# A sigmoid attention with a gated feed-forward: post-sums of the first layers kept in the PSUM banks of products 0 and 1, and two units of products interleaved

## The chip, the core and the metric

The kernel runs on one core of a Trainium2 chip. The metric is the device time of one execution in microseconds; several runs of a kernel are given by their median. A core has TensorE (PE, matmuls into PSUM; PEld is its weight load), VectorE (DVE), ScalarE (ACT), GpSimd (POOL) and SyncE (SP), which here issues all the DMAs. Each engine works through its own queue in order, and semaphores tie the queues together.

## The reference

```python
scores = scale * np.matmul(q, k.transpose(0, 1, 3, 2)) - np.log(S)   # 8 x 12 heads, S = 448, 64 wide
attn = 1.0 / (1.0 + np.exp(-scores))
x = np.matmul(attn, v)                      # brought to 3584 tokens x 768
gate = 1.0 / (1.0 + np.exp(-(x @ w_gate)))  # w_gate, w_val: 768 x 1536
val = x @ w_val
out = gate * val @ w_out                    # w_out: 1536 x 768
```

The feed-forward weights come as 64-bit words and the results are held to the accuracy of fp32.

## The kernel before, in words

**Stages.** The attention runs first (0 to 268.6 us of the span) and leaves x, transposed, in DRAM. Then the first layers (x times w_gate and w_val, 268.6 to 883.7 us), then the second layer (times w_out). Beside them VectorE, ScalarE and GpSimd convert the weights.

**Products.** Both layers work on 2 x 2 blocks with seven products in place of eight (Winograd's form of Strassen). An operand is a sum of blocks, scaled and split into a high and a low fp16 half (`hl`, `hh`, `b`, `whl`), and a product of the first layers is nine matmuls of 128 x 128 by 448 columns: three tiles of the inner dimension, times low-high, high-high and high-low (`product`, L615; matmuls in L625). It fills one of the eight PSUM banks of the pool `un`.

**Units.** A unit is the seven products of one block of w_gate (t = 0) or w_val (t = 1) with one pair of batches. `unit` (L632) gives each product's result to another engine: products 0 and 1 are copied to SBUF by ScalarE (L638, L640); for products 2 and 3 VectorE adds the running sum in SBUF to the bank (u2, u3; `plus`, L610), and GpSimd adds the copy of product 1 to u2 and u3 (u4, c22); products 4, 5 and 6 get one VectorE sum each (c). The four results c and c22 are the blocks of the layer's output. `done` is then called on each: `gate` (L792: ScalarE's sigmoid L794, for two of four a scaling L356) or `value` (L800: gate times value, two on VectorE in L809, two on GpSimd in L811, then a store to DRAM and, two ticks later, ScalarE's row sums of magnitudes, `sum_abs`, L115).

**Visits.** `visits` is a list of (pair of batches, part): four visits with the first four column pairs of the weights (8 units, 56 products each), four with the other two (4 units, 28 products), then the second layers of the four pairs. 48 units in all, 336 products. `a_visit` (L745) calls `tick` after each product; a tick also moves on the loads of the next pair's x (`load_x`), its operands (`split_x`, GpSimd's differences in L326, splits in L356 and L362), the stores, and `beside` (L942): the steps of the weight conversion that a table made from step counts gives to that tick.

**Conversion.** A group of weights is four tiles of words, two steps each (`first`: L218 ScalarE, L199 GpSimd, L200 VectorE; `second`: L209 to L212 VectorE), then its scale, then seven operands (GpSimd's sums in L260, ScalarE's cast in L356, VectorE's rest in L230, the stores). A scale that must hold for all partitions takes the steps of `Scale.steps` (L165): row maximum (`each`, L127), an idle step, a spread by a small matmul (L595), an idle step, the finish. The maximum of the hidden values of the first pair (`OutScale`) is told in the same way at the start of the second layer, where a product is 18 matmuls (`c_visit`, L842).

**Order.** All of this is written out in program order; nothing is moved afterwards. TensorE waits where a bank isn't free, an operand isn't made or a DMA hasn't landed. The weight operands come through a ring of eight buffers (`load_operands`, L426), some of them stay resident in `v` tiles.

## Time and profile before

| | us |
|---|---|
| median of 3 runs (1182.64 to 1185.46) | 1183.63 |
| the profiled execution | 1182.16 |
| its span, first to last instruction | 1180.4 |
| attention | 268.6 |
| first layers, 336 products | 615.1 |
| second layer | 296.7 |
| PE busy / DVE / ACT / POOL | 1135.0 / 872.0 / 644.6 / 628.2 |

The profile is one execution. In its rows an instruction has its line in the kernel, its engine and its operands as out<-in; "idle before" is the engine's time without work ahead of it, and `<-` names what ended that. Matmuls overlap, so the duration of one (353 ns on average) is longer than the distance from one to the next (0.19 us). Of the stages, 490 to 810 us is the part of the first layers in which conversion runs in nearly all ticks.

### The profile page before, as it was taken

The page shows a single profiled execution, that of the slowest core. Times are in us where ns is not written, and L with a number is a line of the kernel's source. Part 1 is how long each engine was busy: PE and PEld are TensorE (multiplying, and loading weights), DVE is VectorE, ACT ScalarE, POOL GpSimd, SP SyncE. Part 2 cuts the span into 40 slices and gives each one's busy share as a digit, 9 for nine tenths or more (in the row PEclk, how much of TensorE's full clock was granted, in tenths as well). Part 3 has the DMA queues.
Part 4 walks back from the last instruction along what each step waited for, and adds up shares of the span by engine and source line. Part 5 has one row for each costly group of instructions (what it writes and reads, how often), then busy time and mean ns, then how long its engine had stood idle before and what let it go on. Part 6 is the DMA issues. An engine that isn't in the chain of part 4 may idle for free.

```text
span 1180.4 us, 20983 instructions
## 1 busy us (share of the span) xinstructions
PE 1135.0 (96%) x7269; PEld 559.0 (47%) x7269; DVE 872.0 (74%) x1414; ACT 644.6 (55%) x1206; POOL 628.2 (53%) x531
## 2 busy tenths in 40 slices
PE   9999999999799999998999898999998999999998
PEld 3434344445355555444545444444554555555554
DVE  4679999634686878888888888887575787686773
ACT  6777577775456656745664555455454335253340
POOL 0255878941574456456444444445477276392850
PEclk9999999999899999999999999999999999999999
DMA  8699788878578637743554789758854786877744
GB/s 291 212 314 332 246 278 273 258 272 271 180 234 280 225 130 264 267 136 106 169 192 151 195 275 302 254 165 276 259 168 146 216 257 203 259 214 235 215 117 152
DMA packets 174251, 265.32 MB, mean 225 GB/s; under 512 B 49216, under 2 KB 150976, under 8 KB 174144
## 3 DMA queue, kind: packets, MB, share of 16 engines
q1 hardware_dynamic: 174144, 263.98, 69.5%
q8 instruction: 57, 0.93, 0.3%
q14 instruction: 50, 0.41, 0.1%
HBM read 182.48 MB, written 81.43 MB: 224 GB/s over the span
## 4 chain that ended last, share of the span: by engine, by line
PE 60%; DVE 15%; POOL 10%; issue 5%; DMA 5%; ACT 4%; SPq 0%; DVEq 0%; POOLq 0%; ACTq 0%
PE un L625 47%; PE av L497 7%; PE sc L472 6%; DVE whl L230 2%; DVE wf L210 2%; POOL wf L260 2%; POOL whl L359 2%; DVE wf L209 2%; DMA v<-ad 2%; DVE wm L211 2%; DVE c L610 1%; POOL v L326 1%; ACT g L794 1%; ACT junk L115 1%; DVE u L610 1%
## 5 line engine op out<-in xcount | busy, mean ns | idle before, releaser
L625 PEld LDWEIGHTS <-A 128*128 128x128 f16 x3024 | 296.2, 98 | 284.5 <-issue 11.0
L625 PE MATMUL un<-b,v 128*128 128x448 f16 x1512 | 310.8, 357 | 15.5 <-ACT p L638 8.2
L625 PE MATMUL un<-b,A 128*128 128x448 f16 x1512 | 304.5, 353 | 5.8 <-DVE c L610 4.1
L625 PE MATMUL un<-hh,A 128*128 128x448 f16 x1008 | 274.3, 354 | 0.0
L625 PEld LDWEIGHTS <-v 128*128 128x128 f16 x1512 | 149.0, 99 | 159.1 <-issue 23.7
L480 ACT ACTIVATE a<-sc,bias 128x896 f32<-128x896 f32 x168 | 169.2, 1008 | 74.9 <-PE sc L472 60.2
L497 PE MATMUL av<-a,v 64*64 64x448 f32 x1344 | 194.6, 540 | 2.8 <-DVE x L514 2.8
L472 PE MATMUL sc<-qk 64*64 64x448 f32 x1344 | 193.3, 539 | 0.4 <-ACT a L480 0.4
L625 PE MATMUL un<-hl,A 128*128 128x448 f16 x504 | 178.3, 354 | 0.0
L610 POOL TENSOR_TENSOR u<-u,p 128x448 f32<-128x448 f32 x48 | 60.0, 1249 | 167.6 <-DVE u L610 135.3
L199 POOL TENSOR_SCALAR wf<-wf 128x384 f32<-128x384 f32 x72 | 41.2, 573 | 183.1 <-ACT wf L218 116.4
L472 PEld LDWEIGHTS sc<-qk 64*64 64x64 f32 x1344 | 66.4, 134 | 77.6 <-issue 63.5
L497 PEld LDWEIGHTS av<-a,v 64*64 64x64 f32 x1344 | 66.5, 133 | 69.1 <-issue 60.8
L115 ACT ACTIVATE junk<-g 128x448 bf16<-128x448 f32 x88 | 50.6, 575 | 77.9 <-DVE g L809 46.8
L794 ACT ACTIVATE g<-c,back 128x448 f32<-128x448 f32 x96 | 62.4, 657 | 48.3 <-DVE c L610 43.8
L326 POOL TENSOR_TENSOR b<-b 128x448 f32<-128x448 f32 x48 | 67.1, 1434 | 38.5 <-DVE hl L362 38.5
L260 POOL TENSOR_TENSOR wf<-wf 128x384 f32<-128x384 f32 x72 | 80.8, 1126 | 0.0
L326 POOL TENSOR_TENSOR v<-v 128x448 f32<-128x448 f32 x48 | 65.8, 1402 | 27.8 <-DVE hl L362 27.8
L610 POOL TENSOR_TENSOR c<-u,p 128x448 f32<-128x448 f32 x48 | 63.1, 1315 | 17.8 <-DVE u L610 15.3
L514 DVE TENSOR_TENSOR x<-av,x 128x448 f32<-128x448 f32 x48 | 29.7, 618 | 49.0 <-ACT x L507 48.4
L811 POOL TENSOR_TENSOR g<-c,g 128x448 f32<-128x448 f32 x44 | 57.3, 1317 | 13.7 <-DVE c L610 13.2
L610 DVE TENSOR_TENSOR c<-un,u 128x448 f32<-128x448 f32 x96 | 57.5, 614 | 8.6 <-PE un L625 5.3
(343 smaller groups left out, 1476.4 us busy)
## 6 DMA issues: line engine op xcount, KB each, us to landing
A<-ad SPq DMA_DIRECT2D x168, 192.0 KB, 3.6
A<-oo SPq DMA_DIRECT2D x168, 192.0 KB, 2.7
qk<-qk SPq DMA_DIRECT2D x23, 896.0 KB, 5.4
h<-g SPq DMA_DIRECT2D x88, 224.0 KB, 2.3
ad<-whl SPq DMA_DIRECT2D x84, 192.0 KB, 4.1
bd<-b SPq DMA_DIRECT2D x30, 448.0 KB, 3.7
b<-bd SPq DMA_DIRECT2D x30, 448.0 KB, 5.8
v<-vv SPq DMA_DIRECT2D x24, 448.0 KB, 4.5
```

The source lines that it names most:

```text
L115: nc.scalar.activation(junk[:, :x.shape[-1]], x, AF.Abs, accum_out=to)
L199: nc.gpsimd.tensor_scalar(out=f, in0=f, scalar1=F32_MAX, scalar2=F64_ZERO, op0=ALU.min, op1=ALU.max)
L260: nc.gpsimd.tensor_tensor(out=x, in0=y, in1=z, op=op)
L326: engine.tensor_tensor(out=to, in0=x, in1=y, op=ALU.subtract)
L472: nc.tensor.matmul(sc[halves[u], h, :S], lhsT=qkt[halves[h], p, k0:k0 + HP], rhs=qkt[halves[h], p, :S], start=True, stop=True)
L480: nc.scalar.activation(a, sc[:, :, :S], AF.Sigmoid, bias=bias, scale=scale)
L497: nc.tensor.matmul(avs[key][halves[h], :S], lhsT=vt[halves[u], g, h], rhs=a[halves[u], h], start=start, stop=g == last)
L514: nc.vector.tensor_tensor(out=x, in0=other, in1=x, op=ALU.add)
L610: engine.tensor_tensor(out=to, in0=x, in1=y, op=ALU.add)
L625: nc.tensor.matmul(acc, lhsT=w, rhs=m, start=i == 0, stop=i == len(terms) - 1)
L794: nc.scalar.activation(gates[i], acc, AF.Sigmoid, scale=units[0])
L811: nc.gpsimd.tensor_tensor(out=h, in0=acc, in1=gates[i], op=ALU.mult)
```

## The change

`unit` becomes a generator that yields after each product. Product 0 opens a bank, `run`; after ScalarE has copied it (p1), product 2 is added by TensorE to the same bank, and ScalarE copies the sum (u2). Product 3 is added to it in turn, and product 6 at last, so that `run` holds the last result itself, which `done` reads from PSUM. Product 1 opens a bank `side`; product 5 is added to it. Product 4 has a bank of its own. Three results take one VectorE sum each: product 4 with p1, `run` after product 3 with p5, `side` after product 5 with u2. GpSimd makes no post-sums. The products of a unit come in the order 0, 1, 2, 4, 3, 5, 6.

`first_layers` takes the units of all visits as one sequence, in which a unit starts seven places after the one before and takes every second place: two units alternate, over the ends of the visits too. The gating, the row sums and the stores are asked for one product later than they were, the loads of x are spread over more ticks, the splits begin one tick earlier, the maximum's spread has one idle step more, and the second layer's start follows that. `Operands` now makes casts as soon as their scale is there.

```diff
--- before.py
+++ after.py
-TAIL = 12
+TAIL = 13
...
+ORDER = (0, 1, 2, 4, 3, 5, 6)
+APART = 2
...
         def steps(self):
-            return [self.rows, idle, self.spread, idle, self.finish]
+            return [self.rows, idle, idle, self.spread, idle, self.finish]
...
-        return 8 * n_groups + lag + (TAIL + 1 if everywhere else TAIL - 2)
+        return 8 * n_groups + lag + (TAIL + 1 if everywhere else TAIL - 3)
...
+    units = [(v_, jp, t) for v_, (kind, _, part) in enumerate(visits) if kind == "A" for jp in JPS_OF_PARTS[part] for t in range(2)]
+    sequence = [(u, at) for _, u, at in sorted((N_OPS * u + APART * at, u, at) for u in range(len(units)) for at in range(N_OPS))]
+    first_unit = [next(u for u, (w_, *_) in enumerate(units) if w_ == v_) for v_ in range(n_a)]
+    starts = [sequence.index((u, 0)) for u in first_unit] + [len(sequence)]
+    def unit_operand(u, at):
+        v_, jp, t = units[u]
+        n, r, part = ORDER[at], N_OPS * (u - first_unit[v_]) + at, visits[v_][2]
+        return (a_dram[jp][t][n].rearrange("p a f -> p (a f)"), [("a", jp, t, n)],
+                (part, r) if resident(part, r) and v_ < n_a - 1 else None)
...
-    wanted = [x for v_ in range(len(visits)) for x in visit_operands(v_)]
+    wanted = [unit_operand(*x) for x in sequence] + [x for v_ in range(n_a, len(visits)) for x in visit_operands(v_)]
     ring, residents, new_resident = [], {}, [None]
...
-    def product(parts):
-        acc = un.tile([P, 512], F32, tag="un", name="un")[:, :S]
+    def product(parts, acc=None):
+        begin = acc is None
+        if begin:
+            acc = un.tile([P, 512], F32, tag="un", name="un")[:, :S]
...
         for i, (w, m) in enumerate(terms):
-            nc.tensor.matmul(acc, lhsT=w, rhs=m, start=i == 0, stop=i == len(terms) - 1)
+            nc.tensor.matmul(acc, lhsT=w, rhs=m, start=begin and i == 0, stop=i == len(terms) - 1, skip_group_check=not begin)
         load_operands()
         after()
         return acc
...
-    def unit(tick, done):
-        def next_product(n):
-            return product([("p (a k f) -> p a k f", [bs[n, k] for k in range(KC)])])
-        p1, p5, u2, u3, u4, c22 = (sb(n) for n in SUMS[:6])
-        nc.scalar.copy(p1, next_product(0))
-        tick()
-        nc.scalar.copy(p5, next_product(1))
-        tick()
-        plus(u2, next_product(2), p1)
-        plus(u4, u2, p5, nc.gpsimd)
-        tick()
-        plus(u3, next_product(3), u2)
-        plus(c22, u3, p5, nc.gpsimd)
-        tick()
-        c = sb(next(cs))
-        plus(c, next_product(4), p1)
-        done(0, c)
-        later.append(lambda: done(3, c22))
-        tick()
-        c = sb(next(cs))
-        plus(c, next_product(5), u4)
-        done(1, c)
-        tick()
-        c = sb(next(cs))
-        plus(c, next_product(6), u3)
-        done(2, c)
-        tick()
+    copies = {n: itertools.cycle(tags) for n, tags in {0: ("p1", "u3"), 1: ("p5", "u4"), 2: ("u2", "c22")}.items()}
+    def unit(b, done):
+        def next_product(n, acc=None):
+            return product([("p (a k f) -> p a k f", [b[n, k] for k in range(KC)])], acc)
+        def copy(n, acc):
+            c = sb(next(copies[n]))
+            nc.scalar.copy(c, acc)
+            return c
+        def sum_of(acc, x):
+            c = sb(next(cs))
+            plus(c, acc, x)
+            return c
+        run = next_product(0)
+        p1 = copy(0, run)
+        yield
+        side = next_product(1)
+        p5 = copy(1, side)
+        yield
+        next_product(2, run)
+        u2 = copy(2, run)
+        yield
+        done(0, sum_of(next_product(4), p1))
+        yield
+        next_product(3, run)
+        done(3, sum_of(run, p5))
+        yield
+        next_product(5, side)
+        done(1, sum_of(side, u2))
+        yield
+        next_product(6, run)
+        done(2, run)
+        yield
...
+        def casts(self, to):
+            while self.cast < min(to, len(self.items)) and self.items[self.cast][:2] in outs:
...
+        def rests(self, at):
+            self.casts(at + 1)
...
-            if 2 <= p < 14 or p >= 14 and p % 2 == 0:
-                next(x_loads, None)
-            if p >= 31:
-                next(splits, None)
-            next(moves, None)
+            if 2 <= p < 20 and p % 3 != 0 or p >= 20:
+                next(self.x_loads, None)
+            if p >= 30:
+                next(self.splits, None)
+            if p == N_OPS and self.keep:
+                self.moves = hold(self.pr, self.jps)
+            if p >= N_OPS:
+                next(self.moves, None)
...
-                    unsent.append((p + 3, h_dram[(pr,) + at], h))
+                    unsent.append((clock[0] + 4, h_dram[(pr,) + at], h))
...
-                unsummed.append((p + 2, h, 4 * at[1] + at[0]))
+                unsummed.append((clock[0] + 3, h, h_sums[pr][:, c:c + 1]))
...
+    def first_layers():
+        going, visit = {}, None
+        for u, at in sequence:
+            v_, jp, t = units[u]
+            if at == 0:
+                if u in first_unit:
+                    if visit:
+                        visit.end()
+                    visit = Visit(v_)
+                going[u] = visit.begin(jp, t)
+            next(going[u])
+            clock[0] += 1
+            send_and_sum()
+            visit.tick()
+        clock[0] += 4
+        send_and_sum()
+        visit.end()
...
-            own = [[], own[1:3], own[3:]]
+            own = [[], [], own[1:4], own[4:]]
```

In the built program ScalarE has 48 instructions more, VectorE and GpSimd 96 fewer each, TensorE and SyncE as many as before. The spread of the maximum of w31 comes after 18 products, before after 17, and the row maximum stands earlier by one to two products.

VectorE, near the end of the fourth visit, before. `un` is a bank, `u2`, `u3` and `u4` the running sums, `p1` a copy, `c` a result, `g` a gate, `w` and `o1s` belong to the weight conversion:

```order
L610 TENSOR_TENSOR u2_7898<-un_7940,p1_7896 128x448
L230 SCALAR_TENSOR_TENSOR whl_7925<-wf_7730,o1s_208,whl_7925 128x384
L209 TENSOR_SCALAR wf_7914<-wf_7914 128x384
L210 SCALAR_TENSOR_TENSOR wf_7914<-wraw_7827,wf_7914 128x384
L211 SCALAR_TENSOR_TENSOR wm_7919<-wraw_7827,wm_7919 128x384
L212 SCALAR_TENSOR_TENSOR wf_7914<-wm_7919,wf_7914 128x384
L610 TENSOR_TENSOR u3_7899<-un_7960,u2_7898 128x448
L610 TENSOR_TENSOR c1_7974<-un_7975,p1_7896 128x448
L809 SCALAR_TENSOR_TENSOR g0_7846<-c1_7974,back3_3315,g0_7846 128x448
L230 SCALAR_TENSOR_TENSOR whl_7958<-wf_7447,o1s_208,whl_7958 128x384
L200 TENSOR_SCALAR wm_7996<-wraw_7923 128x384
L610 TENSOR_TENSOR c0_8004<-un_8005,u4_7900 128x448
```

Every product from 2 on has a bank of its own and a VectorE row that reads it: u2, u3, c1, c0, with the conversion's rows between.

A few products on, at the start of the fifth visit, after. `un_7541` is the bank `run` of one unit, `un_7584` its bank `side`, `un_7791` the bank of product 4 of the unit interleaved with it:

```order
L603 TENSOR_TENSOR c0_7700<-un_7541,u4_7596 128x448
L217 SCALAR_TENSOR_TENSOR whl_7658<-wf_7208,o1s_208,whl_7658 128x384
L196 TENSOR_SCALAR wf_7646<-wf_7646 128x384
L197 SCALAR_TENSOR_TENSOR wf_7646<-wraw_7580,wf_7646 128x384
L198 SCALAR_TENSOR_TENSOR wm_7652<-wraw_7580,wm_7652 128x384
L199 SCALAR_TENSOR_TENSOR wf_7646<-wm_7652,wf_7646 128x384
L603 TENSOR_TENSOR c1_7742<-un_7584,c22_7631 128x448
L217 SCALAR_TENSOR_TENSOR whl_7729<-wf_7393,o1s_208,whl_7729 128x384
L187 TENSOR_SCALAR wm_7767<-wraw_7656 128x384
L825 SCALAR_TENSOR_TENSOR g2_7644<-un_7541,back3_3315,g2_7644 128x448
L603 TENSOR_TENSOR c0_7802<-un_7791,p1_7688 128x448
L217 SCALAR_TENSOR_TENSOR whl_7774<-wf_7480,o1s_208,whl_7774 128x384
```

The first row reads `run` after products 0, 2 and 3, the gating in L825 reads the same bank after product 6, and the rows on u2 and u3 are gone.

ScalarE at the same place, before: the copies out of PSUM in L638 and L640, the gates in L794, the casts and the scalings in L356, the magnitudes in L218 and L115:

```order
L794 ACTIVATE g1_7864<-c1_7848,back3_3315 128x448
L356 ACTIVATE g1_7864<-g1_7864,back3_3315 128x448
L794 ACTIVATE g2_7894<-c0_7880,back3_3315 128x448
L638 COPY p1_7896<-un_7902 128x448
L115 ACTIVATE junk_7917,o2c_209<-wf_7817 128x384
L218 ACTIVATE wf_7914<-wraw_7827 128x384
L356 ACTIVATE whl_7925<-wf_7730,o1s_208 128x384
L640 COPY p5_7897<-un_7927 128x448
L356 ACTIVATE whl_7958<-wf_7447,o1s_208 128x384
```

And after, in the fifth visit, where the copies are L636, the gates L812, the casts and scalings L343, the magnitudes L205 and L102:

```order
L636 COPY u3_7831<-un_7819 128x448
L102 ACTIVATE junk_7833,hc3_3319<-g2_7644 128x448
L812 ACTIVATE g3_7849<-c1_7847,back3_3315 128x448
L343 ACTIVATE g3_7849<-g3_7849,back3_3315 128x448
L102 ACTIVATE junk_7860,o2c_209<-wf_7761 128x384
L205 ACTIVATE wf_7856<-wraw_7771 128x384
L343 ACTIVATE whl_7869<-wf_7208,o1s_208 128x384
L636 COPY u4_7883<-un_7871 128x448
L812 ACTIVATE g1_7900<-c0_7898,back3_3315 128x448
L343 ACTIVATE g1_7900<-g1_7900,back3_3315 128x448
L636 COPY c22_7928<-un_7819 128x448
L812 ACTIVATE g2_7943<-un_7676,back3_3315 128x448
```

`un_7819` is copied after product 0 (to u3) and again after product 2 (to c22), and between the two copies stand gates that wait for VectorE's sums, and casts. The last row takes its gate out of a bank `run` directly.

More of the change, by code (lines that the diff above doesn't have):

```diff
@@ L732, in make @@
+        def rests(self, at):
+            self.casts(at + 1)
+            item = self.items[at]
+            pr, n, k = item
+            rest(hb[item][1], self.source(item), outs[pr, n].by_tile[:, k:k + 1], hb[item][0])
+            b = [hs.get((pr, i, k)) for i in range(4)]
+            for to, x, y in {0: ((0, 1, 0),), 1: ((0, 3, 0), (1, 3, 1)), 2: ((0, 2, 0),)}.get(n, ()):
+                subtract(nc.gpsimd, b[to], b[x], b[y])
         def make(self, to):
             while self.made < min(to, len(self.items) + 2):
-                next(self.maker)
+                if self.made >= 2:
+                    self.rests(self.made - 2)
+                self.casts(self.made)
@@ L930, in sigmoid_attention_glu_kernel @@
     weights = convert(words, halves_of_jps[FIRST:], range(KH), sum_abs, scaled, 1, 1)
[L931 to L933 removed]
     n_one = convert_steps(1, True, 1)
     n_all = 8 * (2 * JPS - FIRST - 1) + convert_steps(KH, False, 1)
[L936 removed]
+    calm = [t for v_ in range(1, n_a - 1) for t in range(starts[v_] + 2, starts[v_] + 30 if v_ < 3 else starts[v_ + 1])]
     due = {}
@@ L950, in before_last @@
         oper[0] = stage.enter_context(tc.tile_pool(name="oper", bufs=1, reuse_waits="tile"))
-    for v_, (kind, *_) in enumerate(visits):
-        (a_visit if kind == "A" else c_visit)(v_)
+    first_layers()
+    for v_ in range(n_a, len(visits)):
+        c_visit(v_)
     stage.close()
```

142 lines of the change are left out of this document (59 added, 83 removed).

## The prediction

> **What bounds the kernel now.** I read the page first: TensorE is busy in 96% of the span, so a change to the other engines can only win what TensorE loses between its matmuls.
>
> ```profile
> span 1180.4 us, 20983 instructions
> PE 1135.0 (96%) x7269; PEld 559.0 (47%) x7269; DVE 872.0 (74%) x1414; ACT 644.6 (55%) x1206; POOL 628.2 (53%) x531
> ```
>
> Next, the pace that TensorE can hold, from the chain that ended last: 504 matmuls, 56 products of nine, with nothing between them.
>
> ```profile
> 315.38 95.34 PE un L625 x504
> ```
>
> That is 95.34 / 56 = 1.7025 us a product. The view by stretches then says where it is not held (columns: length, then busy time and count of PE, PEld, DVE, ACT, POOL, granted clock, DMA).
>
> ```profile
> 268.60:310.00 41.40, 34.18 (x174) 17.23 (x173) 24.37 (x41) 21.34 (x58) 13.66 (x14) 0.92 0.85 281
> 310.00:490.00 180.00, 180.00 (x956) 93.10 (x954) 132.92 (x212) 110.15 (x250) 94.09 (x80) 1.00 0.68 227
> 490.00:810.00 320.00, 295.26 (x1521) 149.22 (x1520) 267.33 (x441) 173.39 (x401) 163.16 (x150) 0.98 0.62 196
> 810.00:883.70 73.70, 73.39 (x390) 37.92 (x388) 46.75 (x78) 38.22 (x81) 39.98 (x33) 1.00 0.76 235
> 883.70:900.00 16.30, 11.75 (x55) 5.58 (x53) 5.15 (x15) 3.99 (x11) 11.50 (x10) 0.90 0.32 97
> ```
>
> The first layers are the first four rows, 615.1 us. Their 336 products at 1.7025 us are 572.0 us, so 43.1 us are lost: at 310 to 490 none, at 490 to 810 (1521 / 9 = 169 products, 287.7 us) 32.3 us, at 268.6 to 310 (174 / 9 products, 32.9 us) 8.5 us, the rest small. The second layers lose 5.9 us at once (16.3 less 55 x 0.189). At stake are 49 us. What TensorE waits for:
>
> ```profile
> PE un L595 <- DVE each L127: 11.0, 4, 7.2
> PE un L625 <- DVE c L610: 10.0, 8, 2.8
> PE un L625 <- ACT p L638: 9.5, 5, 4.6
> PE un L625 <- DVE u L610: 0.7, 1, 0.7
> PE un L595 <- DVE each L127: 4.6, 1, 4.6
> ```
>
> The last row is from the second layers, the others from the first. L595 spreads a maximum over the partitions; L625 is a product that finds no free bank, since all eight still wait for a reader. How late the readers are, a timeline shows:
>
> ```profile
> 635.75 1.87 PE L625 MATMUL un<-b,v 128*128 128x448 f16 x9
> ...
> 652.26 0.51 ACT L638 COPY p<-un 128x448 f32<-128x448 f32 x1
> ...
> 652.83 3.36 PE L625 MATMUL un<-b,v 128*128 128x448 f16 x9 [2.44 <-ACT p L638]
> ...
> 667.49 1.86 PE L625 MATMUL un<-b,A 128*128 128x448 f16 x9 [0.90 <-ACT p L638]
> ```
>
> The product that ended at 637.6 is copied at 652.26, 14.6 us late, and its bank is what the product of 652.83 was waiting for. After that wait nine matmuls take 3.36 us, not 1.87: 1.5 us more at half clock. After 0.90 us of idling nothing of the kind.
>
> Why are they late? VectorE's work in 490 to 810 is 267.3 us for 287.7 us of products, 93%, and it waits besides. One turn of the queues:
>
> ```profile
> 735.55 0.61 DVE L610 TENSOR_TENSOR u<-un,p 128x448 f32<-128x448 f32 x1
> ...
> 736.31 1.14 POOL L610 TENSOR_TENSOR u<-u,p 128x448 f32<-128x448 f32 x1 [3.02 <-DVE u L610]
> ...
> 737.40 1.45 POOL L610 TENSOR_TENSOR c<-u,p 128x448 f32<-128x448 f32 x1
> ...
> 739.40 1.00 POOL L260 TENSOR_TENSOR wf<-wf 128x384 f32<-128x384 f32 x1
> ...
> 740.44 0.62 ACT L356 ACTIVATE whl<-wf,o2s 128x384 f16<-128x384 f32 x1 [3.63 <-POOL wf L260]
> ...
> 741.34 0.95 DVE L230 SCALAR_TENSOR_TENSOR whl<-wf,o2s,whl 128x384 f16<-128x384 f32 x1
> ```
>
> GpSimd waits for VectorE's post-sum, makes two of its own, and only then the weight sum; ScalarE waits 3.63 us for that one, with its copies out of PSUM queued behind, and VectorE's split follows. So the late readers end last here, and their lateness comes from VectorE's load and from this ring of waits.
>
> **The change part by part.** *Post-sums.* Rows by group, 490 to 810:
>
> ```profile
> L610 POOL TENSOR_TENSOR c<-u,p 128x448 f32<-128x448 f32 x24 | 32.1, 1336 | 11.4 <-DVE u L610 11.4
> L610 POOL TENSOR_TENSOR u<-u,p 128x448 f32<-128x448 f32 x24 | 29.7, 1238 | 55.1 <-DVE u L610 41.5 <-ACT p L640 4.6 <-ACT whl L356 3.6
> L809 DVE SCALAR_TENSOR_TENSOR g<-c,back,g 128x448 f32<-128x448 f32 x24 | 25.7, 1069 | 0.9
> L209 DVE TENSOR_SCALAR wf<-wf 128x384 uint32<-128x384 uint32 x32 | 24.7, 771 | 2.2 <-POOL wf L199 2.2
> L610 DVE TENSOR_TENSOR u<-un,u 128x448 f32<-128x448 f32 x24 | 14.9, 619 | 1.3
> L638 ACT COPY p<-un 128x448 f32<-128x448 f32 x23 | 11.8, 513 | 0.0
> ```
>
> Per unit, two VectorE sums go (2 x 0.62 us), both GpSimd sums (1.34 + 1.24), and one ScalarE copy comes (0.51). Over this stretch's 24 units VectorE falls by 29.8 to 237.5 us and GpSimd by 61.8 to 101.4 us; ScalarE rises by 12.3 to 185.7 us, 65% of 287.7. TensorE's matmuls stay as many and as long.
>
> *VectorE beside GpSimd.* The shortest runs of two groups (min/median/max in ns, of the whole program):
>
> ```profile
> L209 DVE TENSOR_SCALAR wf<-wf x72: 344/359/1300, 10.0 to 805.5; 128x384 uint32<-128x384 uint32 x72
> L809 DVE SCALAR_TENSOR_TENSOR g<-c,back,g x44: 685/912/1575, 296.2 to 837.6; 128x448 f32<-128x448 f32 x44
> ```
>
> Against them the means are 0.427 us (x32) and 0.384 us (x24) longer: 22.9 us. If that comes from GpSimd running beside, the 38% of GpSimd's time that leaves (61.8 of 163.2) takes 8.7 us along: VectorE at 228.8 us, 80% of 287.7. At the other end it takes nothing: 83%.
>
> The Trainium skill ("SBUF — State Buffer", Who interferes with whom) goes further: a VectorE instruction with two SBUF inputs is blocked by a GpSimd one that reads SBUF, with one SBUF input it is not. Half of the L809 group now reads PSUM and would drop to 685 ns, 12 x 0.384 = 4.6 us more; by it VectorE is at 78%, and the forecast below 3 us lower. The trace agrees so far as VectorE's sums with one PSUM input hardly vary:
>
> ```profile
> L610 DVE TENSOR_TENSOR c<-un,u x96: 605/612/626, 281.0 to 884.4; 128x448 f32<-128x448 f32 x96
> ```
>
> *What that load costs.* 310 to 490 carries 132.9 us of VectorE in 180, 74%, and loses nothing; 490 to 810 carries 93% and loses 32.3 us. A straight line between the two gives 10 us for 80%. It is my choice of value; the ends are 3 us (the waiting ring is gone) and 32 us (nothing is better). Gain here 22.3 us.
>
> *In-place accumulation and interleaving.* A product that adds to a bank now waits until its reader has finished: products 2, 3 and 6 of each unit, 3 x 48 = 144 handovers. With a unit of the neighbour between, there are three products, 5.1 us, less the read itself (0.51 to 0.62), so readers may be 4.5 us late, where they had eight banks before. Behind a late handover all later products queue. Those products' own readers on ScalarE and VectorE then come later too, and with them the conversion work queued there. Before shows no such wait; that it stays within the 10 us is what I assume. The first unit's start and the last one's end have one product between: 1 us for both, twice at most. Lower bound 0.
>
> *One idle step before the spread.* The spread of w31 comes after product 18, not 17, and its maximum comes one to two products earlier, of which I count one: 3.4 us of the 7.2 us wait. The queue before it is shorter too. I take 6 us of the 8.5 us back (3 to 7). The other three waits, 3.8 us together, lie in 490 to 810 and are in the line above.
>
> *Second layers.* The chain at their start:
>
> ```profile
> 886.04 4.78 POOL L326 TENSOR_TENSOR v<-v 128x448 f32<-128x448 f32 x4
> ...
> 890.77 2.21 POOL L811 TENSOR_TENSOR v<-c,g 128x448 f32<-128x448 f32 x2
> ...
> 895.03 0.23 DVE L127 TENSOR_SCALAR each<-h02m 128x128 bf16<-128x128 f32 x1
> ```
>
> The last gatings stood behind the operand subtractions. Now product 3's value comes before product 5's, and the spread is one product (18 matmuls, 3.4 us) later, with the casts of the third operand behind it. Of 5.9 us I take 4.5 (0 to 5.9), as the casts may be late.
>
> *Moved on the queues.* Three things I cost at nothing:
>
> ```profile
> 0.00:268.60 268.60, 263.81 (x2720) 113.03 (x2720) 195.88 (x384) 191.62 (x224) 160.58 (x143) 0.99 0.81 273
> h<-g SPq DMA_DIRECT2D x88, 224.0 KB, 2.3
> A<-ad SPq DMA_DIRECT2D x168, 192.0 KB, 3.6
> ```
>
> SyncE issues the same number of DMAs. A store of h goes out one product later and lands in 2.3 us; its tile is written again three products, 5.1 us, after the issue, and if the store were held up ScalarE's gate would wait, 1 to 2 us each. The operand loads now come partly two in a row, 3.6 us each, but eight buffers ahead. In the attention the conversions get one more idle step beside a TensorE that is busy for 263.8 of 268.6 us; the last of them end with the same beat, so 0, at most 1 us either way.
>
> Sum: 22.3 + 6 + 4.5 - 1 = 31.8 us. The profiled execution took 1182.2 us (its span and 1.8 us around), the median of the three runs is 1183.6. So 1150.4 by the profile, 1152 by the median.
>
> **The rivals.** *Handovers stall.* If ScalarE and VectorE stay over 4.5 us late, as at 652.26, TensorE pays at each handover. It decides at 0.3 us mean per handover: 144 x 0.3 = 43 us, all that was to be won outside the start and the tail. At 0.5 us, 72 us: 1183.6 - 49 + 6 + 72 = 1213. For it speaks the 14.6 us row; against it that the lateness came with 93% load.
>
> *The ring stays.* GpSimd still makes the weight sums and the gatings, and ScalarE still waits for them in order. Then 490 to 810 loses nearly what it did, less the three spread waits: 1183.6 - 6 - 4.5 - 3.8 = 1169. Against it: 55.1 us of GpSimd's idling in front of the u sums goes.
>
> *Shorter waits, more of them, and the clock.* If in each of the 24 units of that stretch one wait is long enough for the half clock, 24 x 1.5 = 36 us come on top: 1188. The 0.90 us wait without a penalty speaks against it. The Trainium skill ("TensorE: Matmul & The Clock Gate", A second HAM failure mode: psum-queue depth-cycling) describes such swings with micro-idling between groups; the 1.00 clock of 310 to 490 is no such case.
>
> **How the numbers follow.** Forecast case 0.66, ring stays 0.15, handovers stall 0.08, clock 0.04, and 0.07 for a better case, all but 6 us won: 1183.6 - 43 = 1141. About 0.2%, 2.4 us, is what a measurement of this kernel can tell from no change. Faster: 0.66 + 0.15 + 0.07 = 0.88. Of the 0.12 I leave 0.02 to no change, 0.10 to slower. The range takes in the better case, the forecast's bounds and the second rival: 1140 to 1172.
>
> **What would show it.** Right: 490 to 810's products in about 298 us at 80% VectorE; TensorE's waits for ScalarE copies and VectorE sums below 12 us in the first layers; no spread wait over 3 us; ScalarE's wait for the weight sum (3.63 us here) near 1 us. Wrong: TensorE's waits at many products of the run bank, or VectorE still over 90%.

## The result, and the profile after

The kernel after takes 1143.61 us (median of 4 runs, 1142.49 to 1144.12), the kernel before 1183.14 us beside it (4 runs, 1182.28 to 1185.46): a ratio of 0.9662, 95% interval 0.9645 to 0.9678. That is 39.5 us less, where 31.6 were forecast, and inside the range.

The page's first lines, of the kernel after:

```profile
span 1141.8 us, 20650 instructions
...
PE 1124.3 (98%) x7269; PEld 549.3 (48%) x7269; DVE 773.8 (68%) x1318; ACT 663.7 (58%) x1254; POOL 498.2 (44%) x435
```

As many matmuls in 38.6 us less of span; VectorE and GpSimd have lost 98 and 130 us, ScalarE has gained 19. TensorE's pace has not changed, as the chain shows:

```profile
631.84 178.92 PE un L620 x945
```

These are 105 products of 1.704 us without a gap, where the stretch quoted of before had 56 of 1.7025. The view by stretches (length, then busy time and count of PE, PEld, DVE, ACT, POOL, granted clock, DMA):

```profile
268.40:310.00 41.60, 41.60 (x225) 21.52 (x222) 20.94 (x46) 29.13 (x73) 12.00 (x13) 1.00 0.85 288
...
480.00:530.00 50.00, 45.70 (x234) 23.00 (x233) 40.08 (x64) 33.85 (x82) 25.56 (x24) 0.97 0.52 170
530.00:770.00 240.00, 237.89 (x1259) 122.70 (x1258) 173.23 (x331) 149.36 (x345) 73.32 (x78) 1.00 0.74 229
770.00:843.50 73.50, 73.50 (x391) 37.98 (x390) 27.24 (x50) 36.59 (x79) 18.15 (x17) 1.00 0.71 219
843.50:860.00 16.50, 14.90 (x80) 7.61 (x78) 8.79 (x13) 5.90 (x14) 13.47 (x12) 1.00 0.40 114
```

The first layers now last from 268.4 to 851.6, 583.2 us, so 11.2 of the 43.1 us are still lost. The start loses nothing. From 480 to 770 there are 1493 matmuls, 165.9 products or 282.4 us, in 290 us: 7.6 us lost, where that part lost 32.3. VectorE's 213.3 us there are 76% of 282.4, not the forecast 80%. The second layers take 290.2 us in place of 296.7. What TensorE waits for in its products:

```profile
PE un L620 <- ACT c L636: 4.9, 3, 2.8
...
PE un L620 <- DVE c L603: 2.6, 2, 1.6
...
PE un L620 <- ACT u L636: 0.5, 1, 0.5
```

Six waits, 8.0 us, and none in front of a spread. The longest of them, in a timeline of the kernel after (engine, line, operands; in brackets the idle time ahead and what ended it):

```profile
498.24 4.07 POOL L313 TENSOR_TENSOR r<-r 128x448 f32<-128x448 f32 x3
...
498.62 1.29 DVE L196 TENSOR_SCALAR wf<-wf 128x384 uint32<-128x384 uint32 x1
...
499.94 1.38 DVE L197 SCALAR_TENSOR_TENSOR wf<-wraw,wf 128x384 uint32<-128x384 uint32 x1
501.24 1.48 DVE L198 SCALAR_TENSOR_TENSOR wm<-wraw,wm 128x384 uint32<-128x384 uint32 x1
502.76 0.56 DVE L199 SCALAR_TENSOR_TENSOR wf<-wm,wf 128x384 f32<-128x384 uint32 x1
503.23 0.62 DVE L603 TENSOR_TENSOR c<-un,u 128x448 f32<-128x448 f32 x1
...
503.88 0.67 ACT L812 ACTIVATE g<-c,back 128x448 f32<-128x448 f32 x1 [3.62 <-DVE c L603]
...
506.76 0.52 ACT L636 COPY c<-un 128x448 f32<-128x448 f32 x1
...
507.32 1.02 PE L620 MATMUL un<-b,v 128*128 128x448 f16 x3 [2.79 <-ACT c L636]
```

Read it from below. TensorE wants to add to a bank that ScalarE copies only at 506.76. ScalarE had stood for 3.62 us before a gate, for a VectorE sum. That sum came late because, while GpSimd ran its three differences of x (498.24 to 502.3), VectorE's conversion rows took 1.29, 1.38 and 1.48 us. Alone, L196 takes 0.35 and L197 0.56 us. The chain of late readers that the prediction described is still there; it happens less often.

### The profile page after: what moved, and what is told of

Its sections match the earlier page's. It is cut to its first block, busy times and chain, and to the rows that moved or that the text cites. A ratio compares the mean times of both kernels' runs of the same rounds, so it can differ in the third digit from the quotient of the medians.

```text
span 1141.8 us, 20650 instructions
## 1 busy us (share of the span) xinstructions
PE 1124.3 (98%) x7269; PEld 549.3 (48%) x7269; DVE 773.8 (68%) x1318; ACT 663.7 (58%) x1254; POOL 498.2 (44%) x435
## 4 chain that ended last, share of the span: by engine, by line
PE 83%; DVE 6%; issue 3%; POOL 3%; ACT 2%; DMA 2%; SPq 0%; POOLq 0%; DVEq 0%; ACTq 0%
PE un L620 67%; PE av L490 8%; PE sc L465 8%; DVE whl L217 1%; POOL wf L247 1%; DVE wf L197 1%; DVE wf L196 1%; DVE wm L198 1%; POOL whl L346 1%; DVE c L603 1%; DMA p<-xd 1%; POOL wf L186 1%; DMA xd<-x 0%; ACT whl L343 0%; DMA c<-xd 0%
## 5 line engine op out<-in xcount | busy, mean ns | idle before, releaser
L620 PE MATMUL un<-b,v 128*128 128x448 f16 x1512 | 298.1, 354 | 6.4 <-ACT c L636 4.9
L490 PE MATMUL av<-a,v 64*64 64x448 f32 x1344 | 167.1, 540 | 3.7 <-DVE x L507 3.6
L465 PE MATMUL sc<-qk 64*64 64x448 f32 x1344 | 167.1, 541 | 0.4 <-ACT a L473 0.4
L465 PEld LDWEIGHTS sc<-qk 64*64 64x64 f32 x1344 | 55.2, 135 | 77.8 <-issue 65.7
L490 PEld LDWEIGHTS av<-a,v 64*64 64x64 f32 x1344 | 54.2, 134 | 76.4 <-issue 68.8
L812 ACT ACTIVATE g<-c,back 128x448 f32<-128x448 f32 x72 | 47.9, 665 | 67.3 <-DVE c L603 63.7
L603 DVE TENSOR_TENSOR c<-un,u 128x448 f32<-128x448 f32 x72 | 44.7, 621 | 62.4 <-PE un L620 59.9
L313 POOL TENSOR_TENSOR b<-b 128x448 f32<-128x448 f32 x48 | 67.5, 1442 | 40.6 <-DVE hl L349 40.6
L313 POOL TENSOR_TENSOR r<-r 128x448 f32<-128x448 f32 x36 | 44.0, 1231 | 33.1 <-DVE b L349 32.6
L197 DVE SCALAR_TENSOR_TENSOR wf<-wraw,wf 128x384 uint32<-128x384 uint32 x72 | 54.9, 763 | 2.5
L636 ACT COPY p<-un 128x448 f32<-128x448 f32 x48 | 25.3, 526 | 50.5 <-PE un L620 50.5
```

The source lines that it names most:

```text
L197: nc.vector.scalar_tensor_tensor(out=e, in0=raw[:, :, 1], scalar=0xC0000000, in1=e, op0=ALU.bitwise_and, op1=ALU.bitwise_or)
L313: engine.tensor_tensor(out=to, in0=x, in1=y, op=ALU.subtract)
L465: nc.tensor.matmul(sc[halves[u], h, :S], lhsT=qkt[halves[h], p, k0:k0 + HP], rhs=qkt[halves[h], p, :S], start=True, stop=True)
L490: nc.tensor.matmul(avs[key][halves[h], :S], lhsT=vt[halves[u], g, h], rhs=a[halves[u], h], start=start, stop=g == last)
L603: engine.tensor_tensor(out=to, in0=x, in1=y, op=ALU.add)
L620: nc.tensor.matmul(acc, lhsT=w, rhs=m, start=begin and i == 0, stop=i == len(terms) - 1, skip_group_check=not begin)
```

## The experiments

The explanations set against each other are these. **Load**: TensorE loses time because VectorE has too much to do, the prediction's straight line. **GpSimd's reading**: GpSimd's post-sums read SBUF beside VectorE and make VectorE's rows longer at bad moments. **GpSimd's order**: its post-sums wait for VectorE and hold up what is queued behind them, the prediction's ring. **Room**: what counts is how far apart the dependent products are. **The idle step**: the spread has more time.

The table has all runs. "First layers" is the time from their first matmul to the first of the second layers in the profiled execution, in us, and the busy times run from 268.3 us to the same end. The last columns are the mean of one VectorE row of the conversion in the first layers (L209 in before, L196 in after; 344 ns at its shortest) and ScalarE's wait for GpSimd's weight sums in the whole program. The attention, in which no edit adds or takes away work, ends between 265.4 and 268.9 us in these profiles.

| | median us | ratio to before, 95% | first layers | DVE busy | POOL busy | L209/L196 ns | ACT for weight sums |
|---|---|---|---|---|---|---|---|
| before | 1183.14 | | 615.2 | 471 | 311 | 764 | 78.2 |
| after | 1143.61 | 0.9662 (0.9645–0.9678) | 583.2 | 375 | 186 | 601 | 50.9 |
| E1 idle step undone | 1143.40 | 0.9655 (0.9635–0.9674) | 583.1 | 378 | 186 | 601 | 49.0 |
| E2 not interleaved | 1173.57 | 0.9908 (0.9883–0.9933) | 614.6 | 364 | 184 | 545 | 57.5 |
| E3 GpSimd sums put back, waiting | 1164.78 | 0.9835 (0.9816–0.9855) | 607.7 | 411 | 303 | 748 | 83.5 |
| E4 VectorE sums put back | 1150.18 | 0.9716 (0.9687–0.9746) | 594.2 | 428 | 188 | 582 | 56.8 |
| E5 interleaving alone | 1174.30 | 0.9919 (0.9899–0.9939) | 609.8 | 455 | 301 | 887 | 84.9 |
| E7 before, no GpSimd sums | 1150.87 | 0.9722 (0.9696–0.9747) | 586.1 | 425 | 189 | 579 | 42.9 |
| E8 before, no VectorE sums | 1177.33 | 0.9941 (0.9923–0.9960) | 611.1 | 432 | 308 | 907 | 66.9 |
| E9 GpSimd sums, waiting less | 1155.15 | 0.9760 (0.9738–0.9782) | 596.4 | 411 | 286 | 877 | 67.5 |
| E10 GpSimd memsets | 1138.19 | 0.9613 (0.9598–0.9628) | 579.3 | 375 | 272 | 615 | 64.8 |
| E11 before, cast later | 1183.94 | 1.0005 (0.9994–1.0015) | 618.9 | 484 | 313 | 928 | 21.5 |
| E12 after, cast later | 1139.56 | 0.9623 (0.9607–0.9639) | 579.1 | 386 | 190 | 771 | 9.2 |
| E13 before, GpSimd writes only | 1163.20 | 0.9826 (0.9801–0.9851) | 595.1 | 433 | 294 | 641 | 71.9 |

The kernels ran in several groups, each beside its own runs of the kernel before (medians 1183.1 to 1184.8), so differences between groups are taken from the ratios, times 1183.1 us. The mean of the conversion row doesn't by itself order the times: in E12 it is 771 ns and in after 601, and E12 is the faster; in E8 it is 907 and in before 764, and E8 is the faster.

**E1, the idle step undone.** The kernel after with the spread's timing of before.

```diff
-TAIL = 13
+TAIL = 12
...
-            return [self.rows, idle, idle, self.spread, idle, self.finish]
+            return [self.rows, idle, self.spread, idle, self.finish]
...
-        return 8 * n_groups + lag + (TAIL + 1 if everywhere else TAIL - 3)
+        return 8 * n_groups + lag + (TAIL + 1 if everywhere else TAIL - 2)
...
-            own = [[], [], own[1:4], own[4:]]
+            own = [[], own[1:3], own[3:]]
```

> The changed kernel with the extra idle step before the spread taken back, all else kept. Theory (readers were late from VectorE's load and the ring of waits, and both are gone): the spread now finds a short queue, so only the wait of w31 and the one at the second layer's start can come back, 1 to 5 us, 1145 to 1149 us. Rival (the idle step won most of what the spread waits cost, 15.6 us before): 1152 us or more, with waits of L588 on each of 8 us or more in sum.

Measured: 1143.40 us, the same as after, and less than either expectation. One wait before a spread comes back:

```profile
PE un L588 <- DVE each L114: 2.3, 1, 2.3
```

In its place the waits for ScalarE's copies are 2.4 us, not 4.9. The idle step is worth nothing; before, the same number of idle steps went with 15.6 us of such waits. They went with the post-sums: E5, which keeps the extra step and has the post-sums of both engines in SBUF again, has 12.2 us of them, while E3 and E4, with the sums of one engine put back, have 1.0 and 0.4.

```profile
PE un L588 <- DVE each L114: 12.2, 4, 4.9
```

That the maximum is made sooner because the queues are shorter is the likely reason; no run shows it alone. The second layers also take 290.3 us with it undone, so their gain isn't the idle step's either.

**E2, not interleaved.** The kernel after with the products of a unit one behind the other.

```diff
-APART = 2
+APART = 1
```

> The changed kernel with APART = 1: banks kept and added to, but a unit's products one after the other, so that one product (1.7 us) and not three lie between a read and the next product on that bank. Theory: ScalarE's copies start 0.2 to 2.7 us late in the median of a stretch and take 0.5 us, so a handover waits some 0.5 to 1 us in the mean, 144 times: 1200 to 1290 us. Rival (the late readers are simply gone, interleaving buys nothing): 1143 to 1155 us.

Measured: 1173.57 us, between the two expectations. The waits of TensorE for readers of its banks in E2:

```profile
PE un L620 <- ACT u L636: 15.1, 10, 4.2
PE un L620 <- ACT p L636: 8.3, 5, 3.1
PE un L620 <- DVE c L603: 6.9, 6, 1.5
...
PE un L620 <- ACT c L636: 1.1, 2, 0.6
```

This is the rival "handovers stall", made to happen: 23 waits, 31.4 us, the longest 4.2. Each stands before a product 2, 3 or 6, which adds to a bank. Adding to a bank costs that much when the next addition follows too closely (0.2 us a handover in the mean, where 0.5 to 1 were expected), and 8.0 us in all when another unit's products lie between. VectorE has less to do here than in the kernel after (364 us), so load explains nothing of these 31 us.

**E3 and E4, the post-sums put back.** In the kernel after, E3 makes two GpSimd sums a unit that nobody needs (on dead copies, after VectorE's sum of product 3, for which they wait); E4 makes two of VectorE's sums twice.

```diff
         done(3, sum_of(run, p5))
+        plus(p5, u2, p5, nc.gpsimd)
+        plus(p5, u2, p5, nc.gpsimd)
```

```diff
-        def sum_of(acc, x):
+        def sum_of(acc, x, twice=False):
...
+            if twice:
+                plus(c, acc, x)
...
-        done(0, sum_of(next_product(4), p1))
+        done(0, sum_of(next_product(4), p1, True))
...
-        done(1, sum_of(side, u2))
+        done(1, sum_of(side, u2, True))
```

> The changed kernel with two GpSimd sums a unit put back behind VectorE's sum of product 3 (they write a copy that nobody reads any more). 1.25 us each, 48 units, 123 us of GpSimd. Theory (GpSimd's sums stretch VectorE and hold up the weight sums that ScalarE waits for): 7 to 15 us come back, 1150 to 1158 us, and the mean of VectorE's L196 and L825 rises. Rival (only VectorE's own load counts): within 3 us of 1143.6.

> The changed kernel with two VectorE sums a unit put back (products 4 and 5's sums are made twice, 0.62 us each, 60 us in all). Theory (load from 80% back to some 90% in the busy stretch): 5 to 15 us come back, 1149 to 1158 us. Rival (the ring through GpSimd was the cause, VectorE's load was not): within 3 us of 1143.6.

Measured: 1164.78 and 1150.18 us, 20.5 and 6.4 us above after; E3 costs more than either expectation gave it, E4 what was expected. E4's VectorE is busy for longer than E3's (428 us against 411), and it costs a third as much by the medians (its four runs spread over 7.7 us). VectorE's load is not what decides; GpSimd's two sums are. What they wait for, in E3's list of waits:

```profile
POOL p L603 <- DVE c L603: 64.4, 15, 7.5
```

**E5, interleaving alone.** The kernel after with its order of two units, but each product in its own bank and the running sums in SBUF again, on VectorE and GpSimd (products in the order 0, 1, 4, 2, 3, 5, 6).

```diff
-        next_product(2, run)
-        u2 = copy(2, run)
+        plus(p1, next_product(2), p1)
+        plus(u4, p1, p5, nc.gpsimd)
...
-        next_product(3, run)
-        done(3, sum_of(run, p5))
+        plus(p1, next_product(3), p1)
+        plus(p5, p1, p5, nc.gpsimd)
+        done(3, p5)
```

> Interleaving without accumulation in PSUM: the changed kernel with two units alternating, but each product in a bank of its own and the post-sums in SBUF as before (two VectorE sums and two GpSimd sums a unit more, one ScalarE copy less; the sums are made in place, the order of a unit is 0, 1, 4, 2, 3, 5, 6). Theory (the sums that leave the engines are what wins): little is left of the gain, 1165 to 1185 us, with TensorE's waits for banks still some 15 us. Rival (the spreading out by interleaving is what wins): 1143 to 1155 us.

Measured: 1174.30 us, 9.6 below before. So the interleaving alone brings 9.6 us, the banks alone (E2) 10.9, both together 40.0. Of that the first layers get 5.4, 0.6 and 32.0 us in the profiles; most of E2's gain lies in the second layers. Neither half is worth much without the other: E5 keeps GpSimd's sums, E2 lacks the room that the handovers need.

**E7 and E8, the post-sums taken out of the kernel before.** E7 leaves GpSimd's two out: of the result one block lacks product 1, another products 0 and 2. E8 leaves VectorE's two out: products 2 and 3 are computed and not read.

```diff
-        plus(u4, u2, p5, nc.gpsimd)
...
-        plus(c22, u3, p5, nc.gpsimd)
...
-        later.append(lambda: done(3, c22))
+        later.append(lambda: done(3, u3))
...
-        plus(c, next_product(5), u4)
+        plus(c, next_product(5), p5)
```

```diff
-        plus(u2, next_product(2), p1)
-        plus(u4, u2, p5, nc.gpsimd)
+        next_product(2)
+        plus(u4, p1, p5, nc.gpsimd)
...
-        plus(u3, next_product(3), u2)
-        plus(c22, u3, p5, nc.gpsimd)
+        next_product(3)
+        plus(c22, p1, p5, nc.gpsimd)
...
-        plus(c, next_product(6), u3)
+        plus(c, next_product(6), p1)
```

> The kernel before without GpSimd's post-sums (u4 and c22 are not made, the results that need them leave them out). Theory, after the 21 us that GpSimd's sums cost in the changed kernel: 20 to 28 us less than before, 1155 to 1164 us. Rival (in the kernel before VectorE's own load holds everything, GpSimd's sums only cost when handovers are tight): 1175 us or more.

> The kernel before without VectorE's two running sums (u2 and u3 are left out of the results, the banks of products 2 and 3 are not read; GpSimd's sums stay and take p1 in their place, so that they no longer wait for VectorE). Theory: VectorE's 60 us less and GpSimd's wait gone, 10 to 22 us less than before, 1162 to 1174 us. Rival (VectorE's load is the bound): 1150 us or less.

Measured: 1150.87 us, 32.9 less than before, and 1177.33, 7.0 less. E7 wins more than was expected, E8 less. The same answer from the other side: VectorE is busy for 425 us in E7 and 432 in E8, and 26 us lie between them. E7 comes within 7 us of the kernel after with neither banks kept nor units interleaved. E7 also gets 4.1 of the second layers' 6.5 us (292.6 us, in E8 296.0), so their start was held up mostly by GpSimd's post-sums, with the last block coming from one of them.

In E8 GpSimd's sums no longer wait for VectorE. First the kernel before, then E8:

```profile
POOL u L610 <- DVE u L610: 135.3, 24, 24.1
```

```profile
POOL u L610 <- ACT p L640: 128.0, 32, 22.3
```

They wait for ScalarE's copy of product 1 instead, nearly as long. So E8's 7.0 us hold both VectorE's two sums and GpSimd's wait for them, and neither is large in the kernel before as long as GpSimd still makes its own two.

**E9 and E10, occupying GpSimd with and without reading.** Both add work for GpSimd on a dead copy at product 6 of each unit of the kernel after, where it waits less for VectorE than in E3: E9 two sums, E10 four memsets.

```diff
         done(2, run)
+        plus(p5, p5, p5, nc.gpsimd)
+        plus(p5, p5, p5, nc.gpsimd)
```

```diff
         done(2, run)
+        nc.gpsimd.memset(p5, 0.0)
+        nc.gpsimd.memset(p5, 0.0)
+        nc.gpsimd.memset(p5, 0.0)
+        nc.gpsimd.memset(p5, 0.0)
```

> The changed kernel with two GpSimd sums a unit put in at product 6, on a copy that has been free for four products, so that they wait for nobody: GpSimd's load without its wait for VectorE. If the 21 us of the sums behind product 3 came from GpSimd waiting in order (the ring), little stays: 1144 to 1149 us. If they came from GpSimd's load beside VectorE (rows stretched) and from the weight sums queued behind, most stays: 1156 to 1166 us.

> As the run with GpSimd's load at product 6 (1155.2 us), but four memsets a unit in place of the two sums: GpSimd is occupied without reading SBUF. If the 11.5 us came from VectorE's rows being stretched by a GpSimd that reads SBUF (VectorE's busy time rose by 36 us there): no stretch now, 1143 to 1148 us. If they came from the weight sums queued behind on GpSimd, so that ScalarE waits: as far as the memsets take as long as the sums, 1150 to 1156 us.

Measured: 1155.15 and 1138.19 us. GpSimd is busy for 286 and 272 us, nearly alike. The sums cost 11.6 us against after, a little less than the second expectation gave; the memsets win 5.8, which neither expectation had. What VectorE makes of it, by groups, in E9:

```profile
L603 POOL TENSOR_TENSOR p<-p 128x448 f32<-128x448 f32 x48 | 51.4, 1072 | 30.0 <-DVE c L603 28.1
...
L196 DVE TENSOR_SCALAR wf<-wf 128x384 uint32<-128x384 uint32 x44 | 38.6, 877 | 12.3 <-POOL wf L186 9.0 <-DMA A<-ad 3.2
```

and in E10:

```profile
L664 POOL MEMSET p<- 128x448 f32 x24 | 11.7, 489 | 1.4
...
L663 POOL MEMSET p<- 128x448 f32 x24 | 11.3, 472 | 28.5 <-DVE c L603 28.5
...
L196 DVE TENSOR_SCALAR wf<-wf 128x384 uint32<-128x384 uint32 x44 | 27.1, 615 | 10.7 <-POOL wf L186 10.7
```

VectorE's 44 rows of L196 take 877 ns each beside the sums and 615 beside the memsets; its whole time in the first layers is 411 us against 375, the latter exactly that of after. Both wait for VectorE alike too, 28.1 us the sums and 28.5 the memsets (the expectation had them wait for nobody). So it is not that GpSimd is busy or waits, it is what it reads. E3's sums, which wait 64.4 us for VectorE and not 28.1, cost 8.9 us more than E9's, at the same 411 us of VectorE; I put that down to the order, though they also stand beside other rows of VectorE. Why the memsets should win 5.8 us is open (see below).

**E11 and E12, the ring opened on ScalarE.** ScalarE's cast of a weight sum comes one conversion step after GpSimd made the sum, in the kernel before (E11) and in the kernel after (E12).

```diff
-                high(x, sc, to(n))
+                uncast.append((x, sc, to(n)))
...
             split()
+            while uncast:
+                high(*uncast.pop(0))
...
-        return 8 * n_groups + lag + (TAIL + 1 if everywhere else TAIL - 2)
+        return 8 * n_groups + lag + (TAIL + 2 if everywhere else TAIL - 1)
```

The last lines (E11's; E12's are alike) count one step more for each stretch of conversion.

> The kernel before with one thing changed: ScalarE's cast of a weight sum (L356 on whl) is put one conversion step behind GpSimd's sum (L260), two to four products later, so that ScalarE does not stand in front of GpSimd's sum. If ScalarE's wait for that sum (78 us before, 43 us without GpSimd's post-sums) is the way in which GpSimd's sums made the copies late: 15 to 33 us less than before, 1151 to 1169 us. If it is only a sign of it (GpSimd late for other reasons, VectorE stretched): 1175 to 1184 us.

> The same edit on the changed kernel: a version that may beat both. 11 us of TensorE's time in the first layers are still lost there, with ScalarE waiting 51 us for the weight sums. If that wait makes the remaining late copies: 1135 to 1141 us. If it does not: 1142 to 1146 us.

Measured: 1183.94 us, 1.0005 of before, and 1139.56 us. ScalarE's wait for the weight sums falls from 78.2 to 21.5 us in E11, and nothing is won; its place is taken by others:

```profile
PE un L597 <- DVE each L127: 23.3, 7, 9.4
PE un L627 <- DVE c L612: 13.9, 7, 3.4
```

These are TensorE's waits for VectorE, 37 us in place of the 25.6 before, while those for ScalarE's copies went from 9.5 to 1.2. So in the kernel before, taking away the wait that the prediction made half of its case wins nothing. Either it was only a place where lateness showed, or what it cost came back in another way: the edit makes the conversion a step longer, and VectorE's row L209 goes from 764 to 928 ns. E11 doesn't tell the two apart. In the kernel after, the same edit takes 4 us (0.9623 against 0.9662; their intervals just miss each other, and the groups differ): TensorE's waits for ScalarE's copies fall from 5.4 to 1.7 us.

```profile
PE un L622 <- DVE c L605: 3.0, 2, 1.6
PE un L622 <- ACT c L638: 1.7, 2, 1.3
```

E12 does the whole computation and beats both kernels.

**E13, the kernel before with GpSimd writing only.** E3, E9 and E10 were made on the kernel after. To split GpSimd's cost in the kernel before, each post-sum becomes a copy of one column, which keeps the wait and the place, and two memsets, which keep GpSimd busy. Two blocks of the result lack their sums.

```diff
+    def filled(to, x):
+        nc.gpsimd.tensor_copy(to[:, :1], x[:, :1])
+        nc.gpsimd.memset(to[:, 1:], 0.0)
+        nc.gpsimd.memset(to[:, 1:], 0.0)
...
-        plus(u4, u2, p5, nc.gpsimd)
+        filled(u4, u2)
...
-        plus(c22, u3, p5, nc.gpsimd)
+        filled(c22, u3)
```

> The kernel before, in which each of GpSimd's two post-sums of a unit is replaced by a copy of one column of VectorE's sum and two memsets of the rest (left out of the results: products 1, 2 and 3 in two of the four blocks). GpSimd still waits for VectorE's sum in the same place and stays busy for about as long (two memsets of 0.49 us and a copy against 1.13 us, a post-sum's shortest), but reads next to nothing from SBUF. Theory A (what costs is GpSimd reading SBUF beside VectorE): VectorE's time in the first layers falls from 471 to about 430 us and the median comes near that of the kernel before without GpSimd's post-sums, 1151 to 1158 us. Theory B (what costs is GpSimd's queue: its wait for VectorE's sum, and the weight sum behind it): VectorE may fall, the median stays at 1172 to 1184 us, and ScalarE's wait for GpSimd's weight sum stays near 78 us. In between, 1158 to 1172, both carry a part.

Measured: 1163.20 us, 20.6 less than before, between the two expectations: both theories carry a part. VectorE falls to 433 us. Its row L209 in E13, and then in E7, which has no post-sums on GpSimd:

```profile
L209 DVE TENSOR_SCALAR wf<-wf 128x384 uint32<-128x384 uint32 x44 | 28.2, 641 | 12.8 <-POOL wf L199 12.8
```

```profile
L209 DVE TENSOR_SCALAR wf<-wf 128x384 uint32<-128x384 uint32 x44 | 25.5, 579 | 12.1 <-POOL wf L199 12.1
```

In the kernel before it was 764. The reading is worth 20.6 us, if the 17 us less that GpSimd is busy count for nothing. The other 12.3 us to E7 remain while GpSimd still waits for VectorE's sum and stays occupied; ScalarE's wait for the weight sums is still 71.9 us. On the kernel after the same split gave 17.4 us (E9 against E10) and 8.9 us (E3 against E9). The first of these contains the 5.8 us that the memsets win; counted from after itself, E9 is 11.6 of E3's 20.5. So between a half and two thirds of what GpSimd's post-sums cost is their reading, and the rest goes with their place in the order.

## Why the prediction was right, point by point

*The floor and what is at stake.* Right: 1.704 us a product after, and the gain came out of the 49 us. The forecast was 8 us short and inside its range; that it came this near is in part luck, as the fourth point shows.

*Post-sums.* The counts were right. GpSimd's fall over all 48 units is 125 us, for 61.8 in 24; ScalarE's rise is 20 us, for 12.3. VectorE's fall was too small in the sum, because of the next step.

*VectorE beside GpSimd.* The mechanism was right and the size too small. The two groups that the prediction named, over the first layers, in the kernel before:

```profile
L809 DVE SCALAR_TENSOR_TENSOR g<-c,back,g 128x448 f32<-128x448 f32 x44 | 46.8, 1065 | 1.6
...
L209 DVE TENSOR_SCALAR wf<-wf 128x384 uint32<-128x384 uint32 x44 | 33.6, 764 | 12.5 <-POOL wf L199 12.5
```

And in the kernel after:

```profile
L196 DVE TENSOR_SCALAR wf<-wf 128x384 uint32<-128x384 uint32 x44 | 26.4, 601 | 11.2 <-POOL wf L186 8.0 <-DMA A<-ad 3.2
...
L825 DVE SCALAR_TENSOR_TENSOR g<-c,back,g 128x448 f32<-128x448 f32 x22 | 16.6, 755 | 0.8
```

Time above the shortest run fell from 35.2 us (44 rows at 764 - 344 and 44 at 1065 - 685 ns) to 12.9 (44 at 601 - 345 and 22 at 755 - 683): 63% went, where 38% had been counted. Part of the reason is in the other 22 gatings, which now read a bank. The line of the gatings in the kernel after, min/median/max in ns:

```profile
L825 DVE SCALAR_TENSOR_TENSOR g<-c,back,g x22: 683/685/1446, 291.8 to 797.8; 128x448 f32<-128x448 f32 x22
L825 DVE SCALAR_TENSOR_TENSOR g<-un,back,g x22: 671/679/685, 297.5 to 807.5; 128x448 f32<-128x448 f32 x22
```

With both inputs in SBUF one such row may take 1446 ns, with one in PSUM never more than 685. That is what the Trainium skill states ("SBUF — State Buffer", Who interferes with whom), and here the trace agrees. The time that the prediction worked out from it, 3 us lower, was the nearer one, though part of its 4.6 us (38%, 1.8 us) stood already in the 8.7, so that it should have been 2 us.

*What that load costs.* This is the step that fails, though its number came near. "A straight line between the two gives 10 us for 80%": measured are 7.6 us at 76%, where the same line gives 3 us. A load taken too high made up for a line that lies too low, and that is luck. Besides, VectorE's load is not what sets the loss. Busy for 411 us, the time is 1155 (E9) or 1165 (E3); at 425 to 433 us it is 1150 (E4), 1151 (E7), 1163 (E13) or 1177 (E8). What goes with the loss in E3, E7, E9, E10 and E13 is GpSimd's post-sums, and of them more than half their reading of SBUF. The line came near because the change took the sums of both engines away together: VectorE's own two sums are worth 6 to 7 us (E4, E8), GpSimd's two 21 (E3) to 33 (E7). A change that moved only VectorE's work would have been forecast wrong by it: for the 29.8 us of VectorE's two sums in that stretch the line gives about 17.5 us, and E8, which takes them away, wins 7.0.

*In-place accumulation and interleaving.* Right. The handovers cost TensorE 8.0 us of waits in 144, most of the 11.2 us still lost; they lie inside the 10 us left over, as assumed. (Product 5 is added to `side` too, a fourth handover of each unit that the prediction didn't count; seven products lie before it, and TensorE never waits there.) E2 shows that the interleaving decides it: without it they cost 31.4. The prediction held 1 us for start and end; the end alone is 1.6:

```profile
846.26 3.03 DVE L349 SCALAR_TENSOR_TENSOR hl<-v,h01a,hh 128x448 f16<-128x448 f32 x2
...
849.21 0.61 DVE L603 TENSOR_TENSOR c<-un,u 128x448 f32<-128x448 f32 x1
...
849.88 1.86 PE L620 MATMUL un<-b,A 128*128 128x448 f16 x9 [1.60 <-DVE c L603]
```

The last product of the last unit waits for a VectorE sum that stands behind two splits of the second layer's operand.

*One idle step before the spread.* Wrong in its cause: 8.5 us came back where 6 were counted, and none of it is the idle step's (E1). All of it belongs to what the prediction called the shorter queue, as far as is shown.

*Second layers.* 6.5 us for 4.5, 0.6 us beyond its bound. The order of the last blocks was named as the cause; E1, E2, E3, E9 and E10, which all keep it, have 290.3 us there, E5, which has product 3's value before product 5's too but makes it by a GpSimd post-sum, has 295.8. So the order alone doesn't do it. E7 gives 4.1 us of it to GpSimd's post-sums.

*Moved on the queues.* No DMA stands among TensorE's waits. The store of h held up ScalarE's gate once, 2.9 us, and nothing came of it.

*The rivals.* "Handovers stall" needed E2 to appear. "The ring stays" was half right as to ScalarE, whose wait for the weight sums fell only from 78.2 to 50.9 us (the prediction had looked for one near 1 us each; it is 1.8), and wrong as to the price: taking this wait away in the kernel before won nothing (E11). The half clock came once, in the row of 507.32: after 2.79 us of idling the nine matmuls that follow took 3.06 us instead of 1.70, in the timeline matmul by matmul, and the granted clock is 0.50 from 507.6 to 511.0.

The sum of the terms, 31.8 us, fell short of the profile's 38.6 by 2.4 us in the late readers (32.3 - 7.6 against 22.3), 2.5 at the start and 2.0 in the second layers.

*What stays open.* Why four memsets a unit make the kernel after faster by 5.8 us. They delay what is queued behind them on GpSimd and so move its reading to other moments; that this is what wins is only argued. In the profiles E10 is 6.8 us shorter than after, and 3.0 of that lie in the attention, before the first memset; the first layers are 3.9 us shorter. E10 and E12 were not combined. The 12.3 us that remain from E13 to E7 were not split between GpSimd's waiting, its being occupied and the results that go through it. Why VectorE's rows are longer in E8 and E12, which are faster, was not followed up.

## What to carry to other kernels

When an engine is late, don't turn its share of busy time into a loss: put the same work on each of two engines by turns. Here two sums a unit cost 6 us on VectorE, where they take 0.62 us each, and 21 on GpSimd, where they take about 1.25. A wait that is long in the list may only be where lateness shows, so take it away by itself before building a forecast on it (E11 removed 57 us of waiting and won nothing, as other waits took its place). And keeping sums in PSUM pays together with room between the additions to a bank; in the first layers both brought 32.0 us, the banks alone 0.6 and the interleaving alone 5.4.

## What the runs showed of the hardware

Beside GpSimd rows that read two inputs, VectorE rows that read only SBUF can take twice and up to nearly four times as long. Of the 44 rows of L196 in the kernel after's first layers, 30 ran beside no GpSimd row and took 0.352 us on average (at most 0.361); 14 ran beside a GpSimd row with two inputs (a sum, a difference or a product) and took 1.134 (at most 1.300). L196 has only one SBUF input. L197, with two, goes from 0.559 (32 rows) to 1.304 (12 rows). Memsets are another matter. In E10, 15 rows of L197 ran beside memsets alone and took 0.559 us, as if alone; 19 of L196 took 0.495, at most 0.700. VectorE's sums of a bank and a copy (L603) take 0.606 to 0.626 us in the kernel after, beside GpSimd or not. Two of each of L196 and L197, from E10's timeline, beside memsets first and then beside a GpSimd product and a GpSimd sum:

```profile
570.08 0.47 POOL L664 MEMSET p<- 128x448 f32 x1
570.16 0.60 DVE L196 TENSOR_SCALAR wf<-wf 128x384 uint32<-128x384 uint32 x1
...
570.61 0.56 POOL L665 MEMSET p<- 128x448 f32 x1
570.80 0.56 DVE L197 SCALAR_TENSOR_TENSOR wf<-wraw,wf 128x384 uint32<-128x384 uint32 x1
...
578.24 1.43 POOL L831 TENSOR_TENSOR g<-c,g 128x448 f32<-128x448 f32 x1 [3.65 <-DVE c L603]
578.60 1.29 DVE L196 TENSOR_SCALAR wf<-wf 128x384 uint32<-128x384 uint32 x1
...
579.63 1.11 POOL L247 TENSOR_TENSOR wf<-wf 128x384 f32<-128x384 f32 x1
579.92 1.23 DVE L197 SCALAR_TENSOR_TENSOR wf<-wraw,wf 128x384 uint32<-128x384 uint32 x1
```

The Trainium skill ("SBUF — State Buffer", Who interferes with whom) says that a VectorE row with two SBUF inputs contends with a GpSimd one that reads SBUF and not with one that only writes it, and that a row like L196 can run in a mode that takes both ports, in which it contends with GpSimd although it has one input. The runs agree with both, though no row shows the mode itself. The prediction gave the first rule without this exception, and L209 and L196 are cases of it.

The half clock after a wait, over the traces of all fourteen kernels: after TensorE had waited for 1.0 to 2.2 us ahead of a product (with a spread between, both waits together), the nine matmuls took under 2.0 us (1.70 at full clock) in 66 of 67 cases. After 2.2 to 3.4 us they did in 6 of 22, and after longer waits, 3.45 us and more, in none of 17; they then took 2.4 to 3.4 us. So here two short waits cost less than one long one of their sum. The kernel after has one wait above 2.2 us in its products, the kernel before six, by the same count.
